# Weighted sums of both heads of a pair in float32 by column tiles, hash signs by column tiles, and a new table of offsets

## The chip, the cores and the metric

The kernel runs on one core of one Trainium2 chip. The metric is device time in microseconds (us). Three runs of the kernel before gave 755.15, 755.79 and 756.51; the median is 755.79. The profiled execution took 754.8 us, 752.9 of them between its first and last instruction.

## The reference

Attention over hash buckets, and two feed-forward blocks behind it (B = 2, H = 8, S = 768, D = 64, all float32):

```python
q_bits = (einsum('bhsd,dk->bhsk', q, proj) > 0)     # 6 bits, k_bits likewise
mask = q_bucket[..., :, None] == k_bucket[..., None, :]
scores = where(mask, q @ k.T / 8, -1e9)
attn = softmax(scores)                              # 768 x 768 for each of 16 heads
x = (attn @ v) as [1536 tokens, 512]
h = x @ w_in;  x = (h * sigmoid(h)) @ w_out         # 512 -> 2048 -> 512
out = (((x @ w1) * (x @ w2)) @ w3) @ w_out2         # 512 -> 1024 -> 1024 -> 512
```

## The kernel before, in words

**Rounded halves.** TensorE's operands are of a rounded float32 type (`F32R`) in all products. A float32 value is held as a rounded copy ("hi", a `Copy` by ScalarE or GpSimd, or a `tensor_copy`) and the rest ("lo", a subtraction). A product is then three matmuls, hi·hi, hi·lo, lo·hi. The helpers `scaled` (L316 to L320) and `sub` (L323) issue the copies and the subtractions, so many operations have these lines.

**Attention.** The 16 heads go in 8 pairs; a pair's q and k stand with one head in partitions 0 to 63 and the other in 64 to 127. For each pair the kernel loads q, k and v, scales q (`prescale`), splits q and k into hi and lo (`round_`, `rest`), projects onto the hash planes (`project`, L587: twelve matmuls, six for each half of 384 columns, with the planes spread by `place` in `pz`), turns the result into equal-bit marks (`sign`, L591, and `weight`, L604), and gathers for each head the operands of its scores: hi and lo halves stacked to 128 partitions (`qa`, `ka`) and the marks below the last part (`qb`, `kb`, 76 partitions); the gathers are transfers on SP's queue (L527). The first pair ("lone") skips the gathers: its scores are computed by `scores_lone` (L698) in tiles of 64 and then 32 rows of the array, two heads side by side.

A unit is one block of 128 queries of one head. `scores` (L686) gives 128 x 768 scores in PSUM with four matmuls, `peak` (L702, VectorE) the row maximum, `exp` (L708, ScalarE) the exponentials P and their row sums. `turn` (L731) transposes P by six 128 x 128 float32 transposes into two PSUM tiles, three to a tile. Of each tile `split_hi` (ScalarE, pth) makes the rounded copy and `split_lo` (VectorE, L744, ptl) the rest, plus a tiny FLOOR; then the tile is free. There are two such tiles. Three units are a group: `weigh` (L766) multiplies P's halves, 384 columns, by V, in two calls of six matmuls. V's hi and lo (64 columns each, `vhi`, `vlo` on GpSimd) fill the 128 columns together, so one matmul gives a half of P times both halves of V. `move` copies the two 64-partition halves of the result out, and `store` (L781, GpSimd) adds them. At a head's end the row sums are inverted, transposed (`flip`, L793), sent to memory and spread over 64 partitions (`send`, `spread`), and `norm` (L800, GpSimd) multiplies.

**Beside the attention** the product of the last two weight matrices is formed (L832), out of weights that are unpacked and split in "pieces" by ScalarE, VectorE and GpSimd. The **feed-forward part** (L994, L1102, L1146) follows from about 330 us.

**Order.** The kernel is a list of operations (`op`), each with the engines it may run on and an assumed cost, what it depends on, buffers that it takes and gives back, and a due time. A planner (`Plan.run`) goes through them by due time and assigns each its engine and its place there. The table `OFF` shifts due times by the kind of operation and the stage. Assumed costs only set the order; on the chip, every engine goes through its own list and waits for what it needs.

Of the kernel before, what the change touches and what calls it, by code (L numbers as in the profile page):

```python
# [9 lines left out]
F32 = mybir.dt.float32  # L10
# [9 lines left out]
NB = 6  # L20
# [32 lines left out]
    "gate": (0.0, 0.0, -3.05, -34.65, -28.8),
    "gather": (-36.0, -53.0, -10.9, 0.0, 0.0),
    "hand_over": (0.0, 0.0, 45.9, 0.0, 0.0),
    "hi": (-23.3, -23.35, -43.55, -31.85, -15.2),
    "hi_sum": (0.0, 0.0, 3.95, -17.65, -0.55),
    "high": (-15.7, 1.9, -12.3, -15.55, -16.85),
    "invert": (14.5, 17.05, 12.05, 0.0, 0.0),
    "join": (23.5, 14.6, 6.5, 19.0, -2.85),  # L60
    "keep": (0.0, 14.6, -21.3, 0.0, 0.0),
    "lend": (0.0, 0.0, 31.8, 0.0, 0.0),
    "lo": (-21.65, -10.0, -4.85, -17.5, 18.95),
    "lo_sum": (0.0, 0.0, 31.05, 30.9, -3.95),
    "load": (-18.65, -22.1, 6.5, -9.0, -17.2),
    "low": (0.65, 0.5, 2.3, 13.85, 34.75),
    "mark_k": (-29.15, 0.0, 0.0, 0.0, 0.0),
    "marks": (-8.7, 8.9, -47.1, 0.0, 0.0),
    "meet": (0.0, 0.0, 0.0, 0.0, -3.2),
    "more_": (0.0, 0.0, 9.65, 17.15, -20.7),  # L70
    "move": (-12.65, -2.2, -9.85, 0.0, 0.0),
    "norm": (5.5, 5.8, 4.35, 0.0, 0.0),
    "out": (0.0, 0.0, 0.0, 0.0, -7.05),
    "peak": (13.5, 18.95, 24.0, 0.0, 0.0),
    "place": (-25.0, 0.0, 0.0, 0.0, 0.0),
    "prescale": (25.8, 12.7, 0.0, 0.0, 0.0),
    "product": (-44.0, -0.55, 2.15, 0.0, 0.0),
    "project": (-7.15, -0.15, 0.0, 0.0, 0.0),
    "reload": (0.0, 0.0, 0.0, 0.0, 4.85),
    "rest": (1.95, 4.8, 0.0, 0.0, 0.0),  # L80
    "rise": (0.0, 0.0, -18.95, -27.9, -20.5),
    "round_": (46.7, 12.4, 0.0, 0.0, 0.0),
    "scores": (-3.3, -2.55, -3.2, 0.0, 0.0),
    "scores_lone": (-4.2, 0.0, 0.0, 0.0, 0.0),
    "send": (18.0, 31.45, 13.05, 0.0, 0.0),
    "settle": (0.0, -6.55, -4.95, 0.0, 0.0),
    "setup": (9.85, 0.0, 0.0, 0.0, 0.0),
    "side": (-9.3, -34.6, -38.55, 0.0, 0.0),
    "sign": (8.0, 0.6, 36.7, -12.3, -14.5),
    "signed": (7.4, -31.85, 15.05, 0.0, 0.0),  # L90
    "snap": (0.0, 0.0, 16.6, 10.7, 2.05),
    "split_hi": (-2.65, 2.05, 4.2, 0.0, 0.0),
    "split_lo": (-6.35, 13.75, 3.75, 0.0, 0.0),
    "spread": (-8.25, -11.35, 40.85, 0.0, 0.0),
    "squash": (0.0, 0.0, 21.15, 16.95, 5.4),
    "store": (-63.05, -40.8, -42.9, 0.0, 0.0),
    "total": (0.0, 0.0, 17.3, 4.3, -26.85),
    "turn": (-7.7, 0.1, -2.8, 0.0, 0.0),
    "unload": (4.45, -2.55, -4.75, 0.0, 0.0),
    "vhi": (3.05, 0.6, 1.4, 0.0, 0.0),  # L100
    "vlo": (-44.1, -26.65, -5.75, 0.0, 0.0),
    "warm": (0.0, -4.7, 0.0, 0.0, 0.0),
    "weigh": (3.5, 4.6, 4.8, 0.0, 0.0),
    "weight": (3.85, 15.1, 0.0, 0.0, 0.0),
    "x_hi": (0.0, 0.0, -19.75, 0.0, 5.4),
    "x_lo": (0.0, 0.0, 4.9, 0.0, -32.75),
# [27 lines left out]
def pool1(n):  # L134
    return 110 + n
# [134 lines left out]
def lsh_attention_moe_kernel(ctx, tc, qT, kT, v, proj, w3, wo2, win, wo1, w12, rows, out):  # L270
# [205 lines left out]
    sel = const.tile([128, 2], F32, name="sel")  # L476
    pz = ap.tile([128, 2, 2, 128], F32R, name="pz")
    ident = const.tile([128, 128], F32, name="ident")
# [5 lines left out]
    plan.buffers("vraw", tiles(ap, "vraw", [128, 2, NQ, D], F32, 1))  # L484
    plan.buffers("bits", tiles(ap, "bits", [128, S], F32, 1))
# [6 lines left out]
    plan.buffers("pth", tiles(ap, "pth", [128, NQ, GRP * 128], F32R, 2))  # L492
    plan.buffers("ptl", tiles(ap, "ptl", [128, NQ, GRP * 128], F32R, 2))
    plan.buffers("xt", tiles(ap, "xt", [128, GRP * 128], F32, 2))
    plan.buffers("invb", tiles(ap, "invb", [128, S], F32, 1))

    def setup(e):
        nc.vector.memset(pz.bitcast(F32), 0.0)
        for s in score_tiles:
            nc.vector.memset(s[:, :, HF:HF + 1], -BIG / 2)  # L500
        make_identity(nc, ident)

        warm = turns[0]
        for _ in range(18):
            nc.tensor.transpose(warm[:, :128], ident, ident)

    def place(e):

        for side in range(2):
            for j, half in enumerate((up, dn)):  # L510
                cs = slice(64 * side + 32 * j, 64 * side + 32 * j + 2 * NB)
                scaled("ACT", pz[half, side, 0, cs], praw[half])
                sub("POOL", pz[half, side, 1, cs], praw[half], pz[half, side, 0, cs])

# [16 lines left out]
    for n in range(B * NPAIR):  # L531
# [4 lines left out]
        raw, hi, lo = {}, {}, {}  # L536
# [13 lines left out]
        if n == 0:  # L550
            ls = op({"SP": 400}, dma(lambda: sel, lambda: rows), due=lead - 8, size=1024)
            placed = op({"ACT": 800}, place, [lp, begun], due=lead - 7)
        for nm, by in (("q", 0.125), ("k", 1.0)):
# [16 lines left out]
            x = raw[nm]  # L570
            if by != 1.0 and n:
                x = op({"POOL": pool1(S)}, prescale, [x], lead - 1)
# [3 lines left out]
                        [] if lone else [(nm + "lo", key(nm + "lo"))], give=[key(nm + "raw")], port=True)  # L576
        signs, zs = [], []
        for f in range(2):
# [23 lines left out]
        def weight(e, key=key):  # L602
            x = plan[key("bits")]
            engine[e].tensor_scalar(out=x, in0=x, scalar1=sel[:, 1:2], scalar2=1.0, op0=ALU.mult, op1=ALU.mult)  # L604

        wt = None if lone else op({"POOL": pool1(S)}, weight, signs, lead + 9)
        loadv = op({"SP": 400}, dma(lambda key=key: plan[key("vraw")].rearrange("p a b c -> p (a b c)"),
                                   lambda b=b, j=j: v[b, j].rearrange("p a b c -> p (a b c)")),
                   due=lead, take=[("vraw", key("vraw"))], size=393216, kind="fetch_v")
        gathers, marks, vs = [], [], []  # L610
        for par in range(2):
# [22 lines left out]
            else:  # L634
# [10 lines left out]
                for nm, g, x in (("qb", par, mine[2]), ("kb", 2 + par, mine[5])):  # L645
                    mine.append(op({"SP": 400}, dma(
                        lambda nm=nm, hk=hk: plan[hk(nm)][64:64 + 2 * NB].bitcast(F32),
                        lambda g=g, key=key: plan[key("bits")][32 * g:32 * g + 2 * NB]),
                        [wt, x], due + 6, size=36864, kind="marks"))
            gathers.append(mine)  # L650

            def vhi(e, hk=hk, par=par, key=key):
                scaled(e, plan[hk("V")][:, :, 64 * par:64 * par + 64], plan[key("vraw")][:, par])

            def vlo(e, hk=hk, par=par, key=key):
                V = plan[hk("V")]
# [8 lines left out]
        op({"": 0}, lambda e: None, vs, t0, give=[key("vraw")])  # L665
        both = {}
        for par in range(2):
# [3 lines left out]
            o = slice(64 - 64 * par, 128 - 64 * par)  # L671
            exps, weighs, stores = [], [], []
            for i in range(NQ):
# [3 lines left out]
                gk = lambda x, g=u // GRP: (x, "g", g)  # L677
# [37 lines left out]
                else:  # L715
                    sc = both[i] = op({"PE": 500 + 8 * (PE_MORE + HF * PE_COL) if lone else 4 * (PE_MORE + HF * PE_COL)},
# [8 lines left out]
                low = []  # L725
                for g in range(2):
# [523 lines left out]
```

## Time and profile before

| | |
|---|---|
| median of three runs | 755.79 us |
| profiled execution | 754.8 us |
| its span, first to last instruction | 752.9 us |
| busy: PE (matmul) | 726.6 us, 97% |
| busy: PEld (weight load) | 617.9 us, 82% |
| busy: DVE (VectorE) | 589.6 us, 78% |
| busy: ACT (ScalarE) | 451.0 us, 60% |
| busy: POOL (GpSimd) | 305.7 us, 41% |

Matmuls overlap in the array, and their ends are modelled. The time that a stream of them needs is read from one start to the next start (a 512-column matmul shows as 389 ns, but the next starts 227 ns later). Busy shares are averages over the span; the attention part and the feed-forward part differ, so they are read apart.

### The profile page before, as it was taken

How to read it: one execution, taken by the hardware profiler on the slowest of the kernel's cores; microseconds unless marked ns; L12 is line 12 of the kernel's file. 1: busy time of each engine (PE TensorE's matmuls, PEld its weight loads, DVE VectorE, ACT ScalarE, POOL GpSimd, SP SyncE). 2: the span in 40 equal slices, each digit the busy share in tenths (PEclk: the TensorE clock that was granted, in tenths of full speed). 3: DMA queues.
4: the chain of work that ended last, by engine and by line, in shares of the span. 5: the costliest groups of instructions: out<-in, count | busy, mean ns of one | idle time of the engine just before them, and what ended most of it. 6: DMA issues, size and time to landing. Idle time of an engine off the chain costs nothing.

```text
span 752.9 us, 10802 instructions
## 1 busy us (share of the span) xinstructions
PE 726.6 (97%) x3712; PEld 617.9 (82%) x3712; DVE 589.6 (78%) x928; ACT 451.0 (60%) x901; POOL 305.7 (41%) x309
## 2 busy tenths in 40 slices
PE   8988999999999999899999999999999999999997
PEld 6867888888899988778778888888888888888886
DVE  5788788878798988869999979879869766646345
ACT  5778889878888787674865644544445555323110
POOL 5558989978666443253320223023142132200000
PEclk9999999999999999999999999999999999999999
DMA  8946667886555543300431223022100212000004
GB/s 240 210 149 173 199 173 196 192 178 156 134 155 148 155 103 109 95 1 3 138 112 57 86 82 112 18 67 76 65 29 28 66 49 95 16 1 0 1 16 153
DMA packets 27062, 75.97 MB, mean 101 GB/s; under 512 B 4304, under 2 KB 4400, under 8 KB 27008
## 3 DMA queue, kind: packets, MB, share of 16 engines
q1 hardware_dynamic: 27008, 75.29, 36.2%
q8 instruction: 29, 0.48, 0.3%
q14 instruction: 25, 0.20, 0.1%
HBM read 52.44 MB, written 5.29 MB: 77 GB/s over the span
## 4 chain that ended last, share of the span: by engine, by line
PE 76%; DVE 11%; ACT 5%; DMA 3%; POOL 2%; issue 2%; SPq 0%; ACTq 0%; DVEq 0%; POOLq 0%
PE more L1146 17%; PE more L994 14%; PE acc L766 7%; PE turn L731 6%; PE acc L1146 6%; PE more L1102 6%; PE score L686 6%; PE acc L832 5%; PE acc L994 4%; PE acc L1102 3%; DVE st L702 2%; DVE ptl L744 2%; PE acc L587 2%; DVE y L323 2%; DVE piece L323 1%
## 5 line engine op out<-in xcount | busy, mean ns | idle before, releaser
L994 PE MATMUL more<-y,piece 128*128 128x512 f32 x510 | 129.6, 390 | 1.4 <-ACT sg L316 0.8
L744 DVE SCALAR_TENSOR_TENSOR ptl<-turn,pth 128x384 fp32r<-128x384 f32 x192 | 100.9, 549 | 21.1 <-ACT pth L316 20.2
L994 PEld LDWEIGHTS more<-y,piece 128*128 128x128 f32 x510 | 95.3, 188 | 22.9 <-ACT sg L316 1.9
L702 DVE TENSOR_REDUCE st<-score 128x1 f32<-128x770 f32 x96 | 91.1, 953 | 18.5 <-PE score L686 12.9
L316 ACT ACTIVATE pth<-turn 128x384 fp32r<-128x384 f32 x192 | 88.7, 488 | 27.1 <-PE turn L731 26.2
L731 PE MATMUL turn<-ident,P 128*128 128x128 f32 x576 | 86.7, 275 | 7.6 <-DVE ptl L744 6.0
L708 ACT ACTIVATE P<-score,st 128x768 f32<-128x768 f32 x96 | 86.5, 903 | 5.6 <-DVE st L702 4.1
L731 PEld LDWEIGHTS turn<-ident,P 128*128 128x128 f32 x576 | 68.4, 140 | 23.6 <-DVE ptl L744 13.4
L1163 DVE SCALAR_TENSOR_TENSOR X<-more,X 128x512 f32<-128x512 f32 x90 | 61.1, 683 | 16.0 <-PE more L1146 15.4
L766 PE MATMUL acc<-pth,V 128*128 128x384 f32 x192 | 67.5, 352 | 1.2 <-ACT wsb L316 1.2
L766 PE MATMUL acc<-ptl,V 128*128 128x384 f32 x192 | 64.7, 337 | 0.0
L1146 PE MATMUL more<-gh,piece 128*128 128x512 f32 x168 | 59.7, 389 | 0.0
L370 POOL TENSOR_SCALAR t<-raw 128x512 uint32<-128x512 uint32 x30 | 22.2, 740 | 89.7 <-DMA raw<-in_w 22.8
L1102 PE MATMUL more<-x,piece 128*128 128x512 f32 x216 | 54.5, 389 | 0.0
L832 PE MATMUL acc<-piece,piece 128*128 128x512 f32 x192 | 54.3, 406 | 0.0
L686 PE MATMUL score<-ka,qa 128*128 128x384 f32 x168 | 48.6, 370 | 4.2 <-ACT P L708 4.1
L781 POOL TENSOR_TENSOR X<-X,xt 64x384 f32<-64x384 f32 x32 | 33.6, 1049 | 39.0 <-ACT X L316 29.3
L1102 PEld LDWEIGHTS more<-x,piece 128*128 128x128 f32 x216 | 40.5, 188 | 8.4
L316 ACT ACTIVATE sg<-more 128x512 f32<-128x512 f32 x30 | 17.8, 594 | 46.4 <-PE more L994 41.5
L1102 PE MATMUL acc<-x,piece 128*128 128x512 f32 x168 | 41.7, 391 | 2.1 <-DVE qraw L1049 1.2
L686 PE MATMUL score<-kb,qb 76*128 76x384 f32 x168 | 43.6, 341 | 0.0
L366 ACT ACTIVATE t<-raw 128x512 uint32<-128x512 uint32 x42 | 28.2, 674 | 21.7 <-DMA raw<-in_w 7.9
(229 smaller groups left out, 1708.5 us busy)
## 6 DMA issues: line engine op xcount, KB each, us to landing
raw<-in_w SPq DMA_DIRECT2D x32, 512.0 KB
raw<-in_wo SPq DMA_DIRECT2D x24, 512.0 KB
raw<-in_win SPq DMA_DIRECT2D x16, 512.0 KB
ka<-khi SPq DMA_DIRECT2D x28, 192.0 KB
qraw<-in_qT SPq DMA_DIRECT2D x8, 384.0 KB
kraw<-in_kT SPq DMA_DIRECT2D x8, 384.0 KB
vraw<-in_v SPq DMA_DIRECT2D x8, 384.0 KB
invb<-inverse SPq DMA_DIRECT2D x16, 192.0 KB
```

The source lines that it names most:

```text
L316: nc.scalar.activation(out=dst, in_=src, func=AF.Copy, scale=by)
L686: nc.tensor.matmul(out=sc[:, g, :HF], lhsT=lhs[:k, qs], rhs=rhs[:k, g * HF:g * HF + HF], start=(k == 128), stop=(k != 128),)
L702: nc.vector.tensor_reduce(out=plan[uk("st")][:, 0:1], in_=plan[uk("S")][:, :, :HF + 1], op=ALU.max, axis=AX.XY, negate=True)
L708: nc.scalar.activation(out=plan[uk("P")], in_=plan[uk("S")][:, :, :HF], func=AF.Exp, bias=s[:, 0:1], accum_out=plan[hk("sums")][:, i:i + 1],)
L731: nc.tensor.transpose(pt[:, c * 128:c * 128 + 128], P[:, g, c * 128:c * 128 + 128], ident)
L744: nc.vector.scalar_tensor_tensor(out=l, in0=src, scalar=FLOOR, in1=h.bitcast(F32), op0=ALU.add, op1=ALU.subtract)
L766: nc.tensor.matmul(out=xo[:, :N], lhsT=V[:, c, :], rhs=plan[gk(x)][:, c, :], start=(c == 0 and x == "pth"), stop=(c == NQ - 1 and x == "ptl"),
L832: nc.tensor.matmul(out=plan[key + ("ps",)], lhsT=w[:, a, k], rhs=r[:, c], start=(k == 0 and n == 0), stop=(k == 7 and n == 2),)
L994: nc.tensor.matmul(out=plan[bk[b]], lhsT=w[:, a], rhs=y, start=(opens and j == 0 and m == 0), stop=(j == 1 and m == 2), skip_group_check=True)
L1102: nc.tensor.matmul(out=plan[key], lhsT=w[:, a], rhs=x, start=(k == 0 and n == 0), stop=(k == 3 and n == 2))
L1146: nc.tensor.matmul(out=plan[key], lhsT=a, rhs=x, start=(f == 0 and n == 0), stop=(f == 1 and n == 2))
L1163: nc.vector.scalar_tensor_tensor(out=dst, in0=plan[key], scalar=by, in1=dst, op0=ALU.mult, op1=ALU.add)
```

## The change

- **Weighted sums.** P's transposed blocks are no longer split. `evict` copies a tile once, as float32, on ScalarE or VectorE as the planner chooses. `weigh` runs once for both heads of a pair, when the second head's group is complete: V of each head (64 columns, float32, as loaded) goes to its own half of the array's columns, and the two results to the two halves of one PSUM tile. The splits of V, the second copy of `move` and the adds of `store` are gone; `norm` works on both heads at once, on GpSimd or VectorE.
- **Hash signs**, all pairs but the first: raw q and k in float32 are multiplied by the planes, in four column tiles of 32 columns, one for each half of q and of k (`project_tiled`, with `pt` filled by `place_tiled`); one `sign_tiled` of 384 columns takes the place of two, `weight` works on 384 columns, and each head's marks are fetched in four transfers instead of two. The raw q and k are kept until the projection has run.
- **Order.** The assumed costs change with this (also that of `scores_lone`), and all of `OFF` is replaced.

```diff
+    "evict": (7.55, 24.7, 41.35, 0.0, 0.0),
...
-    "turn": (-7.7, 0.1, -2.8, 0.0, 0.0),
+    "turn": (-46.85, -0.5, -0.35, 0.0, 0.0),
...
-    plan.buffers("V", tiles(ap, "V", [128, NQ, 128], F32R, 2))
-    plan.buffers("pth", tiles(ap, "pth", [128, NQ, GRP * 128], F32R, 2))
-    plan.buffers("ptl", tiles(ap, "ptl", [128, NQ, GRP * 128], F32R, 2))
-    plan.buffers("xt", tiles(ap, "xt", [128, GRP * 128], F32, 2))
+    plan.buffers("V", tiles(ap, "V", [128, 2, NQ, D], F32, 2))
+    plan.buffers("pt", tiles(ap, "pt", [128, NQ, GRP * 128], F32, 4))
...
+            def project_tiled(e, key=key):
+                for t in range(4):
+                    nc.tensor.matmul(
+                        out=plan[key("z")][32 * t:32 * t + 32, :HF], lhsT=pt,
+                        rhs=plan[key("qk"[t // 2] + "raw")][:, t % 2 * HF:t % 2 * HF + HF], start=True, stop=True,
+                    )
+            def sign_tiled(e, key=key):
+                nc.vector.tensor_scalar(
+                    out=plan[key("bits")], in0=plan[key("z")][:, :HF], scalar1=0.0, scalar2=sel[:, 2:3],
+                    op0=ALU.is_gt, op1=ALU.is_equal,
+                )
+            zs.append(op({"PE": 150 + 4 * (PE_MORE + HF * PE_COL)}, project_tiled, [*ins, placed_tiled], lead + 6.5,
+                         [("bits", key("bits")), ("W", key("z"))], kind="project"))
...
-        for f in range(2):
+        for f in range(2 if lone else 0):
...
+            op({"": 0}, lambda e: None, [*zs, *lo.values()], lead + 3, give=[key("qraw"), key("kraw")])
...
-                for nm, g, x in (("qb", par, mine[2]), ("kb", 2 + par, mine[5])):
-                    mine.append(op({"SP": 400}, dma(
+                for nm, t, x in (("qb", 0, mine[2]), ("kb", 2, mine[5])):
+                    for f in range(2):
+                        at = 32 * (t + f) + 2 * NB * par
+                        mine.append(op({"SP": 400}, dma(
...
-                    def split_hi(e, views=views):
-                        src, h, l = views()
-                        scaled(e, h, src)
-                    def split_lo(e, views=views):
-                        src, h, l = views()
-                        nc.vector.scalar_tensor_tensor(
-                            out=l, in0=src, scalar=FLOOR, in1=h.bitcast(F32), op0=ALU.add, op1=ALU.subtract
-                        )
+                    def evict(e, uk=uk, mine=mine, g=g, i=i):
...
+                        if e == "ACT":
+                            nc.scalar.activation(out=dst, in_=src, func=AF.Copy, bias=FLOOR)
+                        else:
+                            nc.vector.tensor_scalar_add(dst, src, FLOOR)
...
-                if i % GRP < GRP - 1:
+                if i % GRP < GRP - 1 or par == 0:
                     continue
...
                         for c in range(c0, c0 + 3):
-                            for x in ("pth", "ptl"):
+                            for side in range(2):
                                 nc.tensor.matmul(
-                                    out=xo[:, :N], lhsT=V[:, c, :], rhs=plan[gk(x)][:, c, :],
-                                    start=(c == 0 and x == "pth"), stop=(c == NQ - 1 and x == "ptl"),
+                                    out=xo[64 * side:64 * side + 64, :N], lhsT=V[:, side, c],
+                                    rhs=plan[key(f"pt{side}{grp}")][:, c], start=(c == 0), stop=(c == NQ - 1),
                                 )
-                    xo = op({"PE": 6 * (PE_MORE + N * PE_COL)}, weigh, [*weighs, vs[par], xo], tu + 3,
+                    xo = op({"PE": 150 + 12 * (PE_FREE + N * PE_COL)}, weigh, [*evicted[grp], loadv, xo], tu + 3,
...
-                    scaled(e, plan[gk("xt")][m], plan[gk("xo")][o, :N])
-                    scaled(e, xg, plan[gk("xo")][m, :N])
+                    scaled(e, xg, plan[gk("xo")][:, :N])
...
-            nm = op({"POOL": pool2(S)}, norm, [bc, *stores], te + 20, give=[hk("invb")])
+        nm = op({"POOL": pool2(S), "DVE": dve(S)}, norm, [*spreads, *moves], te + 20, give=[key("invb")], port=True)
```

## Rows read from the trace of the kernel before

**Rows 1.** The page's first part: busy us (share of the span), number of instructions.
```profile
PE 726.6 (97%) x3712; PEld 617.9 (82%) x3712; DVE 589.6 (78%) x928; ACT 451.0 (60%) x901; POOL 305.7 (41%) x309
```
**Rows 2.** Busy us by stretch: bounds, length, engines (instructions), clock, DMA share, GB/s.
```profile
0.00:48.00 48.00, 40.88 (x296) 34.43 (x297) 33.90 (x55) 32.46 (x67) 26.45 (x35) 1.00 0.82 213
48.00:150.00 102.00, 96.04 (x564) 85.36 (x563) 85.17 (x141) 87.17 (x192) 90.58 (x87) 0.98 0.68 182
150.00:340.00 190.00, 182.44 (x1068) 162.95 (x1067) 158.30 (x256) 146.89 (x323) 105.65 (x96) 1.00 0.48 123
340.00:500.00 160.00, 158.57 (x696) 129.99 (x695) 147.15 (x226) 90.66 (x159) 41.26 (x46) 1.00 0.25 79
500.00:748.60 248.60, 248.54 (x1096) 205.13 (x1094) 164.35 (x252) 93.78 (x163) 41.71 (x47) 1.00 0.13 43
```
**Rows 3.** Waits of the weight loads: who <- for whom, us, times, longest.
```profile
PEld turn L731 <- DVE ptl L744: 13.4, 29, 2.0
PEld score L686 <- ACT P L708: 5.4, 5, 2.3
PEld turn L731 <- ACT P L708: 3.2, 3, 1.4
```
**Rows 4.** Timeline at 168.5 us, all engines: start, us, instruction [idle before].
```profile
168.52 0.49 PE L731 MATMUL turn<-ident,P 128*128 128x128 f32 x3
...
168.72 0.96 DVE L702 TENSOR_REDUCE st<-score 128x1 f32<-128x770 f32 x1 [1.00 <-PE score L686]
...
169.09 0.90 ACT L708 ACTIVATE P<-score,st 128x768 f32<-128x768 f32 x1
169.60 0.55 DVE L744 SCALAR_TENSOR_TENSOR ptl<-turn,pth 128x384 fp32r<-128x384 f32 x1
...
170.20 0.55 PE L731 MATMUL turn<-ident,P 128*128 128x128 f32 x3 [1.08 <-DVE ptl L744]
```
**Rows 5.** Timeline of PE at 158.5 us: a group's weighted sums, first and next.
```profile
158.46 0.34 PE L766 MATMUL acc<-pth,V 128*128 128x384 f32 x1
...
160.56 0.82 PE L731 MATMUL turn<-ident,P 128*128 128x128 f32 x6
```
**Rows 6.** Groups of PE by form: count, then busy us, mean ns, idle before.
```profile
L766 PE MATMUL acc<-pth,V 128*128 128x384 f32 x192 | 67.5, 352 | 1.2 <-ACT wsb L316 1.2
...
L587 PE MATMUL acc<-qhi,pz 128*128 128x384 f32 x28 | 10.3, 367 | 0.1
...
L587 PE MATMUL acc<-qlo,pz 128*128 128x384 f32 x14 | 5.0, 358 | 0.0
```
**Rows 7.** Timeline of PE, 24 to 30 us: float32 transposes and row tiles.
```profile
24.01 2.78 PE L522 MATMUL acc<-ident 128*128 128x128 f32 x24
26.63 0.82 PE L731 MATMUL turn<-ident,P 128*128 128x128 f32 x6
27.38 1.31 PE L698 MATMUL score<-x 64*128 64x384 f32 x12
28.63 0.62 PE L698 MATMUL score<-invb,x 12*128 12x384 f32 x4
...
29.80 0.42 PE L766 MATMUL acc<-pth,V 128*128 128x384 f32 x1
```
**Rows 8.** Groups of VectorE, ScalarE and GpSimd by form.
```profile
L744 DVE SCALAR_TENSOR_TENSOR ptl<-turn,pth 128x384 fp32r<-128x384 f32 x192 | 100.9, 549 | 21.1 <-ACT pth L316 20.2
...
L316 ACT ACTIVATE pth<-turn 128x384 fp32r<-128x384 f32 x192 | 88.7, 488 | 27.1 <-PE turn L731 26.2
...
L781 POOL TENSOR_TENSOR X<-X,xt 64x384 f32<-64x384 f32 x32 | 33.6, 1049 | 39.0 <-ACT X L316 29.3 <-DVE X L318 5.2 <-DVE sums L789 3.7
...
L800 POOL TENSOR_TENSOR X<-X,invb 64x768 f32<-64x768 f32 x16 | 29.4, 1838 | 9.2 <-DMA invb<-inverse 8.3
...
L591 DVE TENSOR_SCALAR bits<-acc,sel 128x384 f32<-128x384 f32 x14 | 8.5, 609 | 0.3 <-PE acc L587 0.3
```
**Rows 9.** Transfers of the marks on SP's queue: issue, ns min/median/max, first and last.
```profile
L527 SPq DMA_DIRECT2D qb<-bits x14: 772/787/953, 27.5 to 270.5; - x14
```

More of the change, by code (lines that the diff above doesn't have):

```diff
@@ L63 @@
[L63 to L97, printed above, removed]
@@ L98 @@
-    "turn": (-7.7, 0.1, -2.8, 0.0, 0.0),
[L99 to L106, printed above, removed]
+    "add": (0.0, 0.0, -14.25, -53.9, -17.8),
+    "again": (0.0, 0.0, 2.3, 0.0, 0.0),
+    "aside": (0.0, 0.0, 0.0, 0.0, -4.2),
@@ new lines @@
+    "hand_over": (0.0, 0.0, 25.25, 0.0, 0.0),
+    "hi": (-28.85, -16.5, -45.45, -24.2, -33.5),
+    "hi_sum": (0.0, 0.0, 47.15, -16.6, -12.6),
+    "high": (-37.35, -45.25, -62.3, -64.6, -11.2),
+    "invert": (-40.55, 28.35, -28.55, 0.0, 0.0),
+    "join": (74.1, 73.9, 29.9, 29.65, 17.1),
+    "keep": (0.0, -7.65, -58.95, 0.0, 0.0),
+    "lend": (0.0, 0.0, -30.85, 0.0, 0.0),
+    "lo": (-22.8, -50.8, -9.95, -50.4, 9.6),
+    "lo_sum": (0.0, 0.0, 72.25, 38.5, -2.4),
+    "load": (11.25, 15.35, 40.55, 14.55, 1.0),
@@ new lines @@
+    "low": (25.15, 27.2, 21.35, 63.75, 90.5),
+    "mark_k": (-46.75, 0.0, 0.0, 0.0, 0.0),
+    "marks": (38.3, 22.2, -36.0, 0.0, 0.0),
+    "meet": (0.0, 0.0, 0.0, 0.0, 35.3),
+    "more_": (0.0, 0.0, 16.45, 67.7, 2.75),
+    "move": (-64.7, -26.55, -2.05, 0.0, 0.0),
+    "norm": (0.0, -55.85, -43.25, 0.0, 0.0),
+    "out": (0.0, 0.0, 0.0, 0.0, 18.15),
+    "peak": (22.45, 26.4, 56.2, 0.0, 0.0),
+    "place": (-18.4, 0.0, 0.0, 0.0, 0.0),
+    "place_tiled": (95.0, 0.0, 0.0, 0.0, 0.0),
+    "prescale": (-44.6, -26.85, 0.0, 0.0, 0.0),
@@ new lines @@
+    "product": (-66.85, -7.25, -35.15, 0.0, 0.0),
+    "project": (-30.75, 0.15, 0.0, 0.0, 0.0),
+    "reload": (0.0, 0.0, 0.0, 0.0, 2.35),
+    "rest": (-5.75, 4.15, 0.0, 0.0, 0.0),
+    "rise": (0.0, 0.0, -36.0, -22.2, -30.4),
+    "round_": (47.5, 17.05, 0.0, 0.0, 0.0),
+    "scores": (-2.15, -4.3, 3.25, 0.0, 0.0),
+    "scores_lone": (-15.35, 0.0, 0.0, 0.0, 0.0),
+    "send": (-25.95, 8.85, -72.4, 0.0, 0.0),
+    "settle": (0.0, -7.35, 20.55, 0.0, 0.0),
+    "setup": (-73.25, 0.0, 0.0, 0.0, 0.0),
@@ new lines @@
+    "side": (12.25, -45.9, -77.05, 0.0, 0.0),
+    "sign": (-15.15, 15.7, 8.65, 54.15, 31.6),
+    "signed": (-48.65, -21.55, -39.25, 0.0, 0.0),
+    "snap": (0.0, 0.0, 19.0, 2.9, -1.25),
+    "spread": (-28.2, -30.2, 15.35, 0.0, 0.0),
+    "squash": (0.0, 0.0, 23.8, 20.55, 0.0),
+    "total": (0.0, 0.0, 47.5, -17.95, -6.9),
+    "turn": (-46.85, -0.5, -0.35, 0.0, 0.0),
+    "unload": (3.8, 7.05, 4.6, 0.0, 0.0),
+    "warm": (0.0, 43.75, 0.0, 0.0, 0.0),
+    "weigh": (21.65, 2.6, 99.55, 0.0, 0.0),
@@ L107 @@
+    "weight": (47.0, 0.6, 0.0, 0.0, 0.0),
+    "x_hi": (0.0, 0.0, -14.85, 0.0, 39.05),
+    "x_lo": (0.0, 0.0, -0.2, 0.0, -4.0),
 }
@@ L513, in place, with place_tiled @@
                 sub("POOL", pz[half, side, 1, cs], praw[half], pz[half, side, 0, cs])
+    def place_tiled(e):
+        for j, half in enumerate((up, dn)):
+            scaled(e, pt[half, 2 * NB * j:2 * NB * j + 2 * NB], praw[half])
     begun = op({"DVE": 500}, setup, due=-20)
@@ L535, in lsh_attention_moe_kernel @@
         key = lambda x, n=n: (x, n)
-        raw, hi, lo = {}, {}, {}
+        raw, hi, lo, ins = {}, {}, {}, []
         lone = n == 0
@@ L603, in weight @@
             x = plan[key("bits")]
-            engine[e].tensor_scalar(out=x, in0=x, scalar1=sel[:, 1:2], scalar2=1.0, op0=ALU.mult, op1=ALU.mult)
-        wt = None if lone else op({"POOL": pool1(S)}, weight, signs, lead + 9)
-        loadv = op({"SP": 400}, dma(lambda key=key: plan[key("vraw")].rearrange("p a b c -> p (a b c)"),
+            engine[e].tensor_scalar(out=x, in0=x, scalar1=sel[:, 3:4], scalar2=1.0, op0=ALU.mult, op1=ALU.mult)
+        wt = None if lone else op({"POOL": pool1(HF)}, weight, signs, lead + 9)
+        loadv = op({"SP": 400}, dma(lambda key=key: plan[key("V")].rearrange("p a b c -> p (a b c)"),
                                    lambda b=b, j=j: v[b, j].rearrange("p a b c -> p (a b c)")),
-                   due=lead, take=[("vraw", key("vraw"))], size=393216, kind="fetch_v")
-        gathers, marks, vs = [], [], []
+                   due=lead, take=[("V", key("V"))], size=393216, kind="fetch_v")
+        if not lone:
+            op({"": 0}, lambda e: None, [*zs, *lo.values()], lead + 3, give=[key("qraw"), key("kraw")])
+        gathers, marks = [], []
         for par in range(2):
```

124 lines of the change are left out of this document (52 added, 72 removed).

## The prediction

> **What bounds the kernel now.** I read the page's busy times first, then the stretches, then the waits of TensorE, then a piece of the timeline. The busy times name the engine: the reader is to see PE at 97% of the span, the next engine at 78% [rows 1]. The stretches say where anything is left on it. From 500 to 748.6 us, 1096 matmuls take 248.6 us, which is 0.227 us for each from start to start, and PE has no idle time there; 340 to 500 stands idle for 1.4 of 160 us. Up to 340 us PE is idle for 7.1 + 6.0 + 7.6 = 20.7 us [rows 2]. So the feed-forward part, over half of the span, can give nothing unless PE gets less work there, and the diff takes none away. The whole question lies in the attention part: how much PE work is put in or taken out, and how much of its waiting goes.
>
> The waits of the weight loads show what that waiting is [rows 3]: 13.4 us for the low split of a transposed block (ptl), 29 times, and 5.4 + 3.2 us for the exponentials. (A matmul's end is modelled, so the idle time counted at PE is smaller than this; I use the loads.) The piece of timeline at 168.5 us shows one of them [rows 4]: three transposes end, ScalarE writes their rounded copy, VectorE should write the rest, but a row maximum of 0.96 us is ahead of it in its queue; only after ptl at 169.60 does PE get its transpose tile back, after 1.08 us idle. Two operations, on two engines, one after the other, hold a tile of which there are two.
>
> **The change, part by part.** All sums are made against the profiled execution, 754.8 us (span 752.9, 1.9 around it); the median of the runs shown, 755.79, is 1.0 above it, which I add at the end.
>
> *Weighted sums, PE work.* Before, twelve matmuls of one head's group take from 158.46 to 160.56, 0.175 each [rows 5]; there are two groups of 192 of them (the first stands in [rows 6]), so 67.2 us. Each pass multiplies one rounded half of P by both halves of V side by side in the 128 columns. After, there are 192 matmuls whose operands are float32, two (one for each head) in two 64-column tiles. No row shows a float32 product, only float32 transposes: 24 of 128 columns from 24.01 to 26.63, 0.109 each [rows 7], or 0.85 ns a column where the rounded type takes 0.175/384 = 0.46: two passes. From below that makes 96 pairs × 384 × 0.85 = 31.3 us. My estimate is by what has to be multiplied: the exact product is the same four products of halves that the kernel forms now, each 384 columns at 0.175, so 0.70 us for one matmul. If the two tiles run beside each other, 96 × 0.70 = 67.2 us, the same as before; if they do not, 192 × 0.70 = 134.4. For "beside each other" the nearest row is the first pair of heads, which works in two row tiles: twelve matmuls from 27.38 to 28.63, 1.25 us, where twelve in a row at 0.175 would take 2.10 [rows 7]. I take 67.2, a change of 0 us, and keep -36 and +67 as the ends. The Trainium skill has four passes for true float32 ("FP8 and Floating Point Precision", TensorE Precision Notes); no run here shows it, and by it an estimate is the same 0.70.
>
> *Going into tiles and out.* From the transposes at 26.63 to the first weighted sum at 29.80 are 3.17 us [rows 7]. In it are 12 transposes (1.31) and, at eight pairs of row-tiled matmuls, 8 × 0.175 = 1.40; 0.46 is left for three changes of shape (to 64 rows, to 32, and back), 0.15 each. The weighted sums come in 32 calls of six matmuls; with other work between any two that is 32 × 0.31 = 9.9 us, with each group's two calls adjacent 5.0. I take 9.9, since the list may split them. Here the Trainium skill speaks against the change: "Changing tiling mode (not just tile) drains the TensorE" ("TensorEngine Tiling (Array Packing)", Key Properties). The rows agree, 0.15 us a time; a reader who left it out would forecast 12 us too little with the next part's share.
>
> *Hash signs, PE work.* Removed: two groups of 28 and two of 14 (one of each in [rows 6]), 84 matmuls at 0.175, 14.7 us. Added, for seven pairs: four 32-column float32 tiles at once, 0.70, and 0.31 in and out, so 7.1. Net -7.6; one after another it would be 7 × (2.80 + 0.31) = 21.8, net +7.1. The first pair keeps its old way. PE work in all: 0 + 9.9 - 7.6 = +2.3 us. So the added and the removed work nearly cancel; the gain must come from waiting.
>
> *Eviction.* Removed: 192 ptl on VectorE, 0.549 each, 100.9 us; the 192 copies on ScalarE (0.488) become float32 copies that may run on either engine [rows 8]. A transpose tile is then free after one operation. What is late next: the copy itself can stand behind a maximum (0.96) on VectorE or an exponential (0.90) on ScalarE [rows 4], so I let a quarter of the 13.4 stay and count -10.0. VectorE also loses half of 14 sign operations of 0.609 [rows 8], and both lose moves: 64 of half the partitions become 16. At the copy's price that is about 100 + 4 + 48 × 0.49 = 128 us off two engines. Exponentials come sooner by this: half of 5.4 + 3.2, -4.3. Together -14.3.
>
> *Work at no cost.* GpSimd loses the 32 adds of 1.049 (33.6 us), the splits of V, and eight of 16 normalizations of 1.838 [rows 8]; from 48 to 150 us it is 90.6 of 102 us busy [rows 2], so weight pieces can only come sooner; at PE I count nothing for it. The marks become 56 transfers of 18 KB on SP's queue in place of 28: at 0.787 each, 22 us more issue time over 290 us [rows 9]. Behind them wait the loads of weights and of the next pair. I cost it at nothing since those are requested up to tens of microseconds ahead; without that cover a late mark stops one head's scores for 0.8 us, 14 heads, 11 us. The raw q and k of a pair are kept until the new projection has run, and a group's sums wait for both heads: queued behind them on PE are other heads' transposes and scores, so the last group alone can be late, by 12 × 0.175 = 2.1 us, beside feed-forward work of the first block.
>
> *Sum.* +2.3 - 14.3 = -12.0; 754.8 - 12.0 + 1.0 = 743.8. The order of everything is also new. It can move waits, not PE work; of the waits that remain in the first 340 us (20.7 of idle, of which the 14.3 is a part counted at the loads) I let it take 2 more: 742.
>
> **Rivals.**
> - *Tiles one after another, or partly.* If two column tiles with full 128-row streams do not share the array, the sums cost 134.4 and the signs 21.8: 754.8 + 67.2 + 9.9 + 7.1 - 14.3 + 1.0 = 826. For it: each column tile needs operands of all 128 partitions, where each row tile of the first pair takes 64. Against it: only those row tiles, which overlap fully but for the changes of shape [rows 7]. It decides from the point where a pair takes 0.70 + 12.0/96 = 0.83 us; with a quarter more than full overlap, 1.25 × 0.70 = 0.88, the time is 743.8 + 96 × 0.18 = 761. The Trainium skill's 2.38 times for three column tiles ("TensorE: Matmul & The Clock Gate", Part 3) would make, as an estimate, 0.88; no run here shows it. Chance 0.08 for 826, 0.07 for some 761.
> - *The wait moves to the copy.* Transposes then wait for a ScalarE that runs exponentials of 0.90 and most copies; only 3 us of waiting go. For it: ScalarE already has 87.2 of 102 us from 48 to 150 [rows 2]. Against it: the list can choose VectorE, which has just lost 100 us. 754.8 + 2.3 - 3 + 1.0 = 755. Chance 0.13.
> - *All the named waits go.* -22.0 of the three waits at the loads, calls adjacent (5.0): 754.8 - 2.6 - 22.0 + 1.0 = 731; with the rest of the early idle time down to 724. For it: every helper engine loses load at once. Against it: the first 48 us are idle for 7.1 with transfers on 82% of the DMA engines' time [rows 2], which the change leaves. Chance 0.14.
>
> **How the numbers follow.** Forecast 742, chance 0.58, its own range 734 to 751. About 0.2% (1.5 us) is what a measurement of this kernel can tell from no change. Faster: 0.57 of the forecast, 0.14, and 0.05 of the moved wait, 0.76. Same: 0.01 + 0.05, 0.06. Slower: 0.08 + 0.07 + 0.03, 0.18. The range: 724 from the third rival, 762 from partly shared tiles; left out are 826 and what lies below 724 or between 762 and 826, some 0.17.
>
> **What would show it.** Right: no ptl group; one eviction group of 192 split over ScalarE and VectorE; the wait of transposes for it under 4 us; pairs of weighted sums that start within nanoseconds, 0.70 from pair to pair; PE after 340 us as before. Wrong: the second tile's start 0.7 after the first's; gaps well over 0.15 at each change of shape; PE's idle time up to 340 us still near 20; or new gaps in the feed-forward part, which the new order alone could bring.

## The result, and the profile after

| | before | after |
|---|---|---|
| median | 755.93 us (755.15 to 756.51, four runs) | 735.28 us (734.10 to 737.81, four runs) |
| profiled execution | 754.8 us | 735.99 us |
| its span | 752.9 us | 734.2 us |

The ratio is 0.9732 (95% interval 0.9703 to 0.9760): 20.7 us faster. The forecast was 742, its range 724 to 762.

The busy times of the kernel after, and the granted clock in tenths over 40 slices, from its page:

```profile
PE 717.8 (98%) x3684; PEld 564.3 (77%) x3684; DVE 534.7 (73%) x811; ACT 402.6 (55%) x780; POOL 220.0 (30%) x231
...
PEclk9999999999999999999999999999999999999999
```

PE is busy 8.8 us less [rows 1], the helpers lose much more: 55 us on VectorE, 48 on ScalarE, 86 on GpSimd. The same stretches as in [rows 2] (bounds, length, then PE, PEld, DVE, ACT, POOL with instructions, clock, DMA share, GB/s):

```profile
0.00:48.00 48.00, 43.16 (x312) 32.70 (x312) 29.32 (x49) 30.23 (x65) 19.12 (x28) 1.00 0.80 206
48.00:150.00 102.00, 97.90 (x601) 72.76 (x603) 74.10 (x116) 77.79 (x161) 61.12 (x56) 1.00 0.77 196
150.00:340.00 190.00, 188.09 (x1066) 138.66 (x1062) 139.18 (x201) 127.89 (x263) 57.89 (x57) 1.00 0.47 124
340.00:500.00 160.00, 158.89 (x699) 130.55 (x698) 135.97 (x213) 81.51 (x143) 37.57 (x44) 1.00 0.23 74
500.00:729.90 229.90, 229.25 (x1012) 189.51 (x1011) 155.40 (x233) 85.15 (x151) 44.25 (x50) 1.00 0.14 44
```

PE's idle time up to 340 us falls from 20.7 to 4.8 + 4.1 + 1.9 = 10.8 us. From 500 us on the spacing is as before, 229.9/1012 = 0.227. GpSimd, 90.6 of 102 us busy before from 48 to 150, now has 61. The waits of the weight loads, as in [rows 3]:

```profile
PEld score L697 <- ACT P L719: 6.8, 12, 1.8
PEld turn L741 <- ACT P L719: 4.7, 6, 1.2
PEld turn L741 <- DVE pt L750: 3.0, 6, 1.3
...
PEld turn L741 <- ACT pt L748: 2.1, 7, 0.6
```

Where 13.4 us stood for the low split, 3.0 + 2.1 stand for the copy. The exponentials did not get better: 6.8 + 4.7 against 5.4 + 3.2. The groups of PE and of the two engines that copy, as in [rows 6] and [rows 8]:

```profile
L750 DVE TENSOR_SCALAR pt<-turn 128x384 f32<-128x384 f32 x86 | 45.8, 550 | 30.3 <-PE turn L741 24.3
L770 PE MATMUL acc<-pt,V 128*64 128x384 f32 x384 | 67.7, 493 | 0.1
...
L748 ACT ACTIVATE pt<-turn 128x384 f32<-128x384 f32 x106 | 49.0, 488 | 23.7 <-PE turn L741 22.3
```

The kernel issues 192 float32 matmuls, and the trace has 384 records: each shows as two. What they cost is in PE's timeline, first a call of the weighted sums (the row behind it is the next work), then one pair's hash signs:

```profile
156.40 0.82 PE L741 MATMUL turn<-ident,P 128*128 128x128 f32 x6
157.29 2.16 PE L770 MATMUL acc<-pt,V 128*64 128x384 f32 x12
159.37 0.97 PE L832 MATMUL acc<-piece,piece 128*128 128x512 f32 x3
```

```profile
50.58 0.52 PE L584 MATMUL acc<-qraw,pt 128*32 128x384 f32 x2
50.60 0.52 PE L584 MATMUL acc<-kraw,pt 128*32 128x384 f32 x2
50.93 0.49 PE L584 MATMUL acc<-qraw,pt 128*32 128x384 f32 x2
50.94 0.49 PE L584 MATMUL acc<-kraw,pt 128*32 128x384 f32 x2
51.37 0.44 PE L697 MATMUL score<-ka,qa 128*128 128x384 f32 x1
```

Twelve records in 2.08 us: six pairs, 0.322 from pair to pair (the starts lie 5 to 7 ns apart within a pair) and the rest at the edges. Of the signs four records start within 0.02 us, and 0.35 later the other four. So tiles do run beside each other; a float32 matmul takes 2 x 0.322 = 0.644 us.

**The account.** I give every matmul its spacing from start to start (0.227 for 512 columns, 0.175 for 384, 0.109 for a transpose, 0.161 for a record of the weighted sums, 0.0805 for one of the tiled signs); what is left up to the last start is the stays in column tiles and waiting. A stay is a stretch of matmuls in column tiles, with other work before and behind it: 7 of signs and 26 of sums, since the list puts a group's two calls next to each other in 6 of 16 groups. It costs some 0.09 before its first record, 0.15 behind its last and 0.11 at the first matmul after it. The other matmuls are the same in number; their 626.3 holds some 1.9 for the first pair's changes of shape.

| us | before | after | change |
|---|---|---|---|
| weighted sums | 67.2 | 61.8 | -5.4 |
| hash signs of seven pairs | 14.7 | 4.5 | -10.2 |
| going into column tiles and out | 0 | 11.6 (33 stays, 0.35 each) | +11.6 |
| the rest: waiting, start | 40.1 | 25.9 | -14.2 |
| all other matmuls | 626.3 | 626.3 | 0 |
| from the span's start to the last matmul's start | 748.3 | 730.0 | -18.3 |

The two profiled executions are 18.8 apart, the medians 20.7.

### The profile page after: what moved, and what is told of

Its sections match the earlier page's. It is cut to its first block, busy times and chain, and to the rows that moved or that the text cites. A ratio compares the mean times of both kernels' runs of the same rounds, so it can differ in the third digit from the quotient of the medians.

```text
span 734.2 us, 10401 instructions
## 1 busy us (share of the span) xinstructions
PE 717.8 (98%) x3684; PEld 564.3 (77%) x3684; DVE 534.7 (73%) x811; ACT 402.6 (55%) x780; POOL 220.0 (30%) x231
## 4 chain that ended last, share of the span: by engine, by line
PE 78%; DVE 11%; ACT 4%; DMA 3%; issue 2%; POOL 1%; SPq 0%; DVEq 0%; ACTq 0%; POOLq 0%
PE more L1146 17%; PE more L994 13%; PE acc L770 8%; PE turn L741 7%; PE score L697 7%; PE acc L832 6%; PE acc L1146 5%; PE more L1102 5%; PE acc L1102 4%; PE acc L994 3%; DVE piece L320 2%; DVE t L373 2%; PE score L709 2%; ACT P L719 1%; DVE st L713 1%
## 5 line engine op out<-in xcount | busy, mean ns | idle before, releaser
L994 PE MATMUL more<-y,piece 128*128 128x512 f32 x498 | 122.9, 390 | 1.2 <-DVE sg L1010 0.6
L1163 DVE SCALAR_TENSOR_TENSOR X<-more,X 128x512 f32<-128x512 f32 x92 | 61.7, 685 | 22.1 <-PE more L1146 21.7
L750 DVE TENSOR_SCALAR pt<-turn 128x384 f32<-128x384 f32 x86 | 45.8, 550 | 30.3 <-PE turn L741 24.3
L770 PE MATMUL acc<-pt,V 128*64 128x384 f32 x384 | 67.7, 493 | 0.1
L1146 PE MATMUL more<-gh,piece 128*128 128x512 f32 x174 | 63.6, 390 | 0.1
L1102 PE MATMUL more<-x,piece 128*128 128x512 f32 x252 | 62.6, 390 | 0.4 <-DVE kraw L1049 0.4
L748 ACT ACTIVATE pt<-turn 128x384 f32<-128x384 f32 x106 | 49.0, 488 | 23.7 <-PE turn L741 22.3
L1102 PEld LDWEIGHTS more<-x,piece 128*128 128x128 f32 x252 | 47.2, 188 | 10.6 <-DVE kraw L1049 0.8
L770 PEld LDWEIGHTS acc<-pt,V 128*64 128x64 f32 x384 | 25.2, 136 | 31.0 <-issue 29.3
L832 PEld LDWEIGHTS acc<-piece,piece 128*128 128x128 f32 x192 | 32.9, 188 | 15.7 <-issue 10.1
L1146 PEld LDWEIGHTS more<-gh,piece 128*128 128x128 f32 x174 | 32.7, 188 | 7.3 <-DVE X L1163 0.5
```

What stands on the lines that cost most here:

```text
L748: nc.scalar.activation(out=dst, in_=src, func=AF.Copy, bias=FLOOR)
L750: nc.vector.tensor_scalar_add(dst, src, FLOOR)
L770: nc.tensor.matmul(out=xo[64 * side:64 * side + 64, :N], lhsT=V[:, side, c], rhs=plan[key(f"pt{side}{grp}")][:, c], start=(c == 0), stop=( ...
L832: nc.tensor.matmul(out=plan[key + ("ps",)], lhsT=w[:, a, k], rhs=r[:, c], start=(k == 0 and n == 0), stop=(k == 7 and n == 2),)
L994: nc.tensor.matmul(out=plan[bk[b]], lhsT=w[:, a], rhs=y, start=(opens and j == 0 and m == 0), stop=(j == 1 and m == 2), skip_group_check=True)
L1102: nc.tensor.matmul(out=plan[key], lhsT=w[:, a], rhs=x, start=(k == 0 and n == 0), stop=(k == 3 and n == 2))
```

## Experiments

Each was timed beside the kernel before on the same chip (medians 755.0 to 755.7 there); the changed kernel, run again on the second of the three chips, took 736.06 (ratio 0.9743, 0.9718 to 0.9768). That run was put on record with this:

> The changed kernel as it is, on the chip of the three runs beside it: 733 to 738 us.

**The tiles side by side: their price.** Both heads in the same columns:

```diff
-  out=xo[64 * side:64 * side + 64, :N], lhsT=V[:, side, c],
+  out=xo[:64, :N], lhsT=V[:, side, c],
-  rhs=plan[key(f"pt{side}{grp}")][:, c], start=(c == 0), stop=(c == NQ - 1),
+  rhs=plan[key(f"pt{side}{grp}")][:, c], start=(c == 0 and side == 0), stop=(c == NQ - 1 and side == 1),
...
-  scaled(e, xg, plan[gk("xo")][:, :N])
+  for half in (up, dn):
+      scaled(e, xg[half], plan[gk("xo")][up, :N])
```

> The changed kernel with the weighted sums of both heads in the same 64 columns and the same half of the PSUM tile (the result holds the sum of the two heads, copied to both halves by two operations of 64 partitions). Same instructions on PE, same lists, nothing can run beside another. Theory: the 192 matmuls take 0.644 each one after another, 123.6 us in place of 61.8: 790 to 802 us with 16 copies more. Rival: part of it hides in time in which PE waits: under 780 us.

796.93 us, ratio 1.0543 (1.0529 to 1.0556): 61.7 above the changed kernel, as forecast from 192 x 0.644 - 61.8 = 61.8. In PE's timeline 23 records of two calls (one is missing from the trace) now take almost twice what 24 take in the changed kernel, which stands below it:

```profile
144.71 7.63 PE L770 MATMUL acc<-pt,V 128*64 128x384 f32 x23
```

```profile
148.81 4.09 PE L770 MATMUL acc<-pt,V 128*64 128x384 f32 x24
```

Without sharing, and with these 16 copies more, the change would have lost 41 us. This is the mechanism of the first rival of the prediction, for the sums alone. It put 67.2 us on them; they cost 61.7, since a matmul takes 0.644, not 0.70. The signs one after another were not tried.

**The order within a call.** Three matmuls of one head, then three of the other:

```diff
-  for c in range(c0, c0 + 3):
-      for side in range(2):
+  for side in range(2):
+      for c in range(c0, c0 + 3):
```

> The changed kernel with the six matmuls of a call of the weighted sums in another order: three of one head, then three of the other, in place of one of each in turn. Every instruction stays, only neighbours in PE's queue change. Theory: two tiles run beside each other only where neighbours in the queue lie in different tiles. A float32 matmul takes 0.644 us (two records of 0.322), so a call takes 6 x 0.644 - 0.322 = 3.54 us in place of 3 x 0.644 = 1.93, and 32 calls add 51 us: 780 to 792 us. Rival: PE's queue or its waiting hides the order (a later matmul of the free tile goes ahead): 734 to 740 us.

751.09 us, ratio 0.9949 (0.9931 to 0.9968): 15.8 above the changed kernel. Both theories missed. The timeline of two adjacent calls (24 records, then the next work):

```profile
154.66 4.79 PE L770 MATMUL acc<-pt,V 128*64 128x384 f32 x24
159.38 0.97 PE L832 MATMUL acc<-piece,piece 128*128 128x512 f32 x3
```

4.72 us from start to next, where the changed kernel needs 4.03 and two calls strictly in order would take 7.08. So the second head's matmuls started before the first head's earlier ones in the queue were through: the two streams overlap, but the second begins and ends about two records (0.70 us) late, once for each stay of the sums. By the account the edges of the 33 stays grow from 11.6 to 29.6 us, 0.70 at each of the 26 of sums and nothing at the seven of signs; waiting gives 3.2 back in the profiled execution. Neighbours in the queue should lie in different tiles, but a few of one head in a row do not cost the whole overlap.

**Hash signs as before**, the rest as after:

```diff
-  zs.append(op({"PE": 150 + 4 * (PE_MORE + HF * PE_COL)}, project_tiled, ...
-  for f in range(2 if lone else 0):
+  for f in range(2):
```

> The changed kernel with the hash signs of the kernel before: twelve matmuls of a pair with rounded halves and two sign operations, no column tiles of 32, marks in two transfers a head. Theory: PE's work is what counts, 14.7 us against 4.5 plus seven times 0.355 for the changes of shape, so +7.7 us, and up to 3 more by VectorE's seven extra operations: 742 to 747 us. Rival: the signs lie in time in which PE waits anyway: 734 to 738 us.

746.47 us, ratio 0.9879 (0.9848 to 0.9911), 11.2 above the changed kernel, in the range of the theory. In the profiled executions 10.4 us: +10.2 of array work, -3.9 of stays (21 in place of 33), +4.1 of waiting. But this list was planned anew, and as much waiting stands at one place of the feed-forward part, behind the last of the weighted sums (295.9 us):

```profile
310.81 0.49 PE L1124 MATMUL more<-qhi,piece 128*128 128x512 f32 x1 [2.65 <-ACT qhi L313]
311.94 0.80 PE L1124 MATMUL more<-qlo,piece 128*128 128x512 f32 x1 [0.64 <-DVE qlo L320]
```

From 311.26 to 318.09 us the granted clock was at 1.2 GHz besides, up to 3.4 us of lost work; the changed kernel has neither. So 6.3 us (10.2 - 3.9) are shown to be the signs', some 30% of the whole gain; that the waiting belongs to them is not shown.

**The old table of offsets** in the changed kernel:

```diff
-    "evict": (7.55, 24.7, 41.35, 0.0, 0.0),
-    "exp": (-9.4, -8.0, 8.7, 0.0, 0.0),
+    "evict": (-2.65, 2.05, 4.2, 0.0, 0.0),
+    "exp": (-1.1, 1.75, 15.6, 0.0, 0.0),
...
```

> The changed kernel with the table of offsets of the kernel before (the copy out of the transpose tiles takes the old value of the rounded copy, the new filling of the planes takes 0). Theory: the gain of 20.7 us is array work (15.6 us less from first to last matmul, less 11.6 us for going into tiles and out) and waiting of PE (14.2 us less), and the new table has a part in the last alone. Array work and changes of shape stay; of the waiting a third comes back: 737 to 745 us. Rival: the new table is the gain, the rewritten parts cancel out: 750 to 758 us.

735.48 us, ratio 0.9736 (0.9705 to 0.9767): the same as with the new table, to within the 2.3 us of its interval. Neither theory: the new table has no measurable part in the gain. The planned costs and the operations themselves are enough.

**Taking the low split from the kernel before**, in two ways; in both, GpSimd fills the low tiles with zeros once, near the start, and the matmuls stay. First the operation is gone from the list and all is planned anew:

```diff
-  low.append(op({"DVE": dve(HF)}, split_lo, [a], tu + 1.5, give=[uk(f"T{g}")]))
+  low.append(op({"": 0}, lambda e: None, [a, zeroed], tu + 1.5, give=[uk(f"T{g}")]))
```

> The kernel before without the 192 low splits of transposed P on VectorE: the low half is left out of the result (its tiles hold zeros, filled once by GpSimd), all matmuls stay. So the array's work is that of before (708 us), the transpose tile is free after one operation, and VectorE has 101 us less to do. Theory: the waiting of PE for the low split (13.4 us at the weight loads) and half of that for the exponentials go, 9 to 15 us: 741 to 747 us. Rival: the waiting moves to the copy on ScalarE or to another engine, and the time stays at 752 to 756 us.

758.32 us, ratio 1.0037 (1.0008 to 1.0065): nothing gained, against my theory. Other waits stand in their place, for the signs at the weight loads, and in the timeline one for an accumulator tile:

```profile
PEld acc L594 <- DVE bits L598: 3.7, 3, 1.4
```

```profile
138.57 0.87 PE L839 MATMUL acc<-piece,piece 128*128 128x512 f32 x3
142.38 0.66 PE L594 MATMUL acc<-qhi,pz 128*128 128x384 f32 x1 [2.94 <-ACT wsb L316]
142.83 0.52 PE L594 MATMUL acc<-qlo,pz 128*128 128x384 f32 x1
143.15 0.52 PE L594 MATMUL acc<-qhi,pz 128*128 128x384 f32 x1
```

The clock has a part too: ten runs had a mean granted clock of 0.983 to 0.995, the kernel before beside them 0.995 to 0.999.

So the second keeps all lists and does not issue the instruction:

```diff
   def split_lo(e, views=views):
-      nc.vector.scalar_tensor_tensor(out=l, in0=src, ...)
+      pass
...
+  for x in ptls:
+      nc.gpsimd.memset(x.bitcast(F32), 0.0)
```

> The kernel before with every engine's list as it was, except that the 192 low splits of transposed P are planned but not issued (the low half is left out of the result; its tiles hold zeros, written by GpSimd in the first 10 us). Unlike the earlier run without them, the list is not planned anew. All matmuls stay. Theory: that run gained nothing because the new list moved other work into the way; with the old list the 13.4 us at the weight loads go and the exponentials come sooner: 741 to 748 us. Rival: in the kernel before PE waits for other things as soon as these are gone (the two accumulator tiles, the signs): 751 to 756 us.

752.97 us, ratio 0.9956 (0.9936 to 0.9976): 3 us. The waits of its weight loads:

```profile
PEld score L689 <- ACT P L711: 8.5, 10, 2.3
PEld turn L734 <- ACT pth L316: 3.1, 4, 1.5
...
PEld turn L734 <- ACT P L711: 2.0, 3, 1.2
```

The 13.4 us for the low split are gone, 3.1 for the copy are left; the exponentials now cost 8.5 + 2.0 in place of 5.4 + 3.2. By the account its rest is 34.9 in place of 40.1: 5.2 us in that execution, 3 in the medians. Its ten runs fall into two groups by the mean granted clock: three at 0.995 to 0.997 took 749.4, seven at 0.989 to 0.992 took 752.4 to 756.2, and the kernel before had 0.994 to 1.0 beside them. So a lower clock takes part of what the low split gives. The median is in the rival's range: a good part of the named wait only covered another. And the loads named too much to begin with: before the matmuls themselves, the kernel before waits less for the low split:

```profile
PE turn L731 <- DVE ptl L744: 6.0, 9, 1.6
```

**Putting the load back into the kernel after.** Every copy on ScalarE, and a second one by VectorE that frees the tile; or the second one out of SBUF, so that it only loads VectorE:

```diff
-  a = op({"ACT": act(HF), "DVE": dve(HF)}, evict, ..., [uk(f"T{g}")])
+  a = op({"ACT": act(HF)}, evict, ..., [])
+  op({"DVE": dve(HF)}, again, [a], tu + 1.5, give=[uk(f"T{g}")])   # first: reads the transpose tile
+  # second: gives the tile after evict; again reads and writes pt in SBUF
```

> The changed kernel with the load of before on the helpers of a transposed tile: every copy out of it on ScalarE, and behind it a second one of the same values by VectorE, which alone frees the tile (192 more of some 0.55 us). PE's work is that of the changed kernel. Theory one (the gain in waiting comes from the tile that is freed after one operation and from VectorE's 100 us): 10 to 15 us come back, 745 to 751 us. Theory two (after the run in which the low split was taken from the kernel before and nothing was gained: the waiting went with other work, such as the splits of V and the signs): 735 to 740 us.

> As the run with every tile copied twice, but the second operation reads the copy in SBUF and writes the same values back, so the transpose tile is free after ScalarE's copy; VectorE has about the same 192 operations more. If holding the tile is what costs: 735 to 740 us. If VectorE's load is what costs: as the run with every tile copied twice, 745 to 751 us.

802.88 us (ratio 1.0648, 1.0617 to 1.0679) and 785.99 us (1.0405, 1.0382 to 1.0428): far beyond either theory. The stretches of the first and of the second, and the waits of the first:

```profile
48.00:150.00 102.00, 89.57 (x482) 59.37 (x482) 71.62 (x117) 75.50 (x162) 66.38 (x62) 0.95 0.70 179
150.00:340.00 190.00, 166.82 (x912) 114.48 (x908) 136.72 (x229) 124.99 (x278) 39.03 (x38) 0.94 0.47 123
```

```profile
48.00:150.00 102.00, 83.21 (x444) 59.02 (x442) 88.82 (x116) 70.22 (x151) 69.90 (x60) 0.90 0.66 167
150.00:340.00 190.00, 171.91 (x1032) 123.09 (x1030) 163.30 (x249) 134.73 (x303) 56.98 (x48) 0.98 0.49 132
```

```profile
PEld turn L741 <- DVE pt L759: 38.3, 85, 1.9
PEld score L697 <- ACT P L719: 34.0, 43, 1.7
```

The waits for the tile (38.3) and for the exponentials (34.0, in the second run 37.3) are there, and the clock adds to them: a mean of 0.95 of 102 us and 0.94 of 190 is some 33 us at 1.2 GHz, up to 16 us of lost work. But the kernel before carried this load too and took 755. Both lists were planned anew with a table that was not made for them, so the 67 and the 50 us are not the price of the low split; the two runs show that the load can cost this much, not what it cost.

**All copies on ScalarE**, lists kept:

```diff
-  if e == "ACT":
-      nc.scalar.activation(out=dst, in_=src, func=AF.Copy, bias=FLOOR)
-  else:
-      nc.vector.tensor_scalar_add(dst, src, FLOOR)
+  nc.scalar.activation(out=dst, in_=src, func=AF.Copy, bias=FLOOR)
```

> The changed kernel with all 192 copies out of the transpose tiles on ScalarE, at the places of its lists (86 were on VectorE). ScalarE gets 42 us more, VectorE 47 less. Theory: a transpose tile is free after one operation on either engine, but on ScalarE this one stands behind exponentials of 0.90, so the waits at the transposes grow by 5 to 15 us: 740 to 752 us. Rival: VectorE's load alone sets the waits, and they shrink: 732 to 736 us.

744.76 us, ratio 0.9854 (0.9831 to 0.9877): 9.5 above the changed kernel, in the range of the theory.

```profile
PEld turn L741 <- ACT pt L747: 13.2, 27, 1.0
```

The wait for the copy grows from 5.1 (both engines) to 13.2. With these lists, that the copy may go to either engine is a real part of the gain; without it the second rival of the prediction (the wait moves to the copy, 755) comes true by about half.

**Fewer stays.** Both calls of a group in one, planned anew (`range(0, NQ, 6)`), and then with the lists kept, the first call issuing nothing:

```diff
-  for c in range(c0, c0 + 3):
+  for c in range(NQ if c0 else 0):
```

> The changed kernel with the two calls of a group's weighted sums put into one (24 records in a row, never split). The list splits them in 10 of 16 groups, so there are 26 stays in the column tiles; at 0.355 us for each stay the ten that go save 3.6 us. Theory: 2 to 5 us under the changed kernel on the same chip. Rival: a block of 4 us keeps scores and transposes behind it, ScalarE and VectorE run dry, and the time is the same or up to 3 us longer.

> The changed kernel with its lists as they are, except that the first of a group's two calls of the weighted sums issues nothing and the second issues all 24 records. No call is planned anew, only six matmuls move back to their neighbours. Theory: ten stays in the column tiles fewer at 0.355 us, and the loss of the run with one planned call came from its list: 731 to 735 us beside 735 to 736 of the changed kernel. Rival: blocks of 4 us starve ScalarE and VectorE whatever the list: 738 to 748 us.

748.32 us (ratio 0.9904, 0.9885 to 0.9923) and 740.43 us (0.9803, 0.9772 to 0.9833); the changed kernel has 0.9743. No gain in either; the theory missed twice, and the second run's median is in the range of its rival (738 to 748). In the second the edges fall from 11.6 to 7.9 us, 3.7 for ten stays as forecast, but waiting grows from 25.9 to 28.9 in its profiled execution (735.3), and the other runs reach 746. The first shows what a new list does: its rest without the stays is 35.5, and up to 3.4 of that is the clock (6.8 us at 1.2 GHz). No version beat the changed kernel.

## Why the prediction was right

- *Weighted sums, array work.* Forecast 0, measured -5.4. The step "the same four products of halves that the kernel forms now, each 384 columns at 0.175" fits: the trace shows two records of 0.322, not passes, but 0.644 is four times 0.161, so it was right but for the price of one, 0.161 in place of 0.175. Both ends, -36 and +67, were excluded by the spacing.
- *Into tiles and out.* Forecast 12.1 (39 stays at 0.31), measured 11.6 (33 at 0.35): fewer stays, each dearer. The estimate from the row tiles of the first pair held for column tiles. The sentence of the Trainium skill that a change of tiling mode drains the array ("TensorEngine Tiling (Array Packing)", Key Properties) agrees with the 0.35 us a stay.
- *Hash signs.* Forecast -9.8 without the stays, measured -10.2.
- *Eviction.* Forecast -14.3 and 2 more by the order; the waiting fell by 14.2. The sum was right, its reason only in part: that the two agree is luck. Two steps were wrong. "I let a quarter of the 13.4 stay and count -10.0": taken alone from the kernel before, the low split gives 3 us in the medians and 5.2 in the profiled execution, since 13.4 at the loads was 6.0 at the matmuls and the exponentials were late next. "Exponentials come sooner by this: half of 5.4 + 3.2": they cost 11.5 at the loads now. What made up for it lies in part outside the three named waits, between 300 and 400 us, where the feed-forward part takes over; the stretch in the kernel before, in the kernel after, and in the kernel before without the low split (lists kept):

```profile
300.00:400.00 100.00, 95.23 (x429) 77.41 (x428) 86.49 (x131) 67.84 (x127) 33.21 (x31) 1.00 0.21 67
300.00:400.00 100.00, 98.89 (x434) 80.91 (x433) 92.55 (x139) 63.78 (x115) 31.87 (x34) 1.00 0.24 79
300.00:400.00 100.00, 96.17 (x431) 78.17 (x430) 85.14 (x127) 65.98 (x124) 34.37 (x33) 1.00 0.21 68
```

  PE's idle time there fell from 4.8 to 1.1 us, and only to 3.8 without the low split. In the kernel before, products of that part waited at the loads for VectorE, which has 55 us less to do now:

```profile
PEld more L1102 <- DVE y L323: 1.7, 1, 1.7
PEld acc L1102 <- DVE qraw L1049: 1.5, 1, 1.5
PEld acc L1102 <- DVE kraw L1049: 1.2, 1, 1.2
```

  So of the 14.2, some 5 are the low split, some 3 more lie in that stretch, and up to 2 are the clock: [rows 2] has 0.98 from 48 to 150, some 4 us at 1.2 GHz, and the stretch after has 1.00. Which of the removed operations ended its waits was not isolated, and neither were the other 4 or 5 us (the splits of V, the moves and adds, half the normalizations, the signs, one sum for two heads). Such parts need not add up.
- *Order.* I let it take 2 us; the run with the old table shows none, but its interval is no narrower than that.
- *Work at no cost.* The four transfers of marks a head made no wait at PE that the list of waits names, and from 500 us on the feed-forward part kept its spacing, as forecast. But I took all idle time up to 340 us for the attention's; the first product of the feed-forward part stands at 295.7 us in the kernel before, and the 3.7 us above are mostly in its waits.
- *Rivals.* Unshared tiles were excluded by the spacing of 0.322 and priced at 61.7 us for the sums. The wait did move to the copy, but only by 5.1 us; the sign "under 4 us" was missed. That all named waits go was too much: 16.6 us of the kind still stand.

The forecast was 6.7 us above the median, mostly the 5.4 of the weighted sums.

## What to carry to other kernels

Where a product is built of rounded halves side by side, plain float32 in column tiles does the same array work, and the work of making halves is gone; it pays best if the tiles' matmuls follow each other in turn (three of one head first left 4 of the 20 us), and if stays in the tiles are long enough for 0.35 us each. The wait with the largest number is not what its removal gives: look for what would be late next, and try it with the lists kept, since the two edits that were tried both ways took 5 and 8 us longer with a new list.

## What was not expected of the hardware

- A float32 matmul of 384 columns shows as two records 0.322 us apart, each with its own weight load (0.136 us for 64 columns).
- Two column tiles are two streams: with one head's three matmuls ahead of the other's, the second stream began 0.70 us late and then kept pace. The Trainium skill has matmuls start and end strictly in program order ("TensorE: Matmul & The Clock Gate", Part 3, The mechanism); 4.72 us for two calls, where that order would make 7.08, speaks against it for tiles, and the measurement decides. (The trace does not list the queue; that it holds the matmuls in the kernel's order is taken for granted.)
- After the wait of 2.94 us in the re-planned run without the low split, the matmuls that follow stand 0.32 apart in place of 0.175: TensorE had done nothing for that time, and the granted clock was at 1.2 GHz from 141.79 to 148.62 us. Such a wait cost more than its length; in the run with the old signs the same stands behind the wait of 2.65 us.
